# A hand-planned attention and gated-MLP kernel: set-up chain, last additions, turned tiles and the choice of plan

## Chip, core and metric

The kernel runs on one core of a Trainium2 chip. The metric is device time in microseconds of one execution. Engines are called TensorE (PE in the profile), VectorE (DVE), ScalarE (ACT), GpSimd (POOL) and SyncE (SP, which issues nearly all DMAs). PEld is TensorE's weight load.

## What is computed

Four batches, eight heads, 768 positions, head size 64. Attention keeps the keys that are among the first 8 or at most 95 positions back, with a bias by distance; its output, 768 x 512 per batch, is the x of a gated MLP with f32 weights that arrive as float64 or float32.

```python
scores = scale * q @ k.T - slope[head] * dist        # masked unless global or local
a = softmax(scores);  x = a @ v                      # (B, S, 512)
h = gelu(x @ w_in);   u, v = h[..., :512], h[..., 512:]
v_n = (v - mean(v)) / sqrt(var(v) + 1e-6) * g_ln
gated = u * (einsum('ts,bsd->btd', w_sg, v_n) + b_sg)
out = x + gated @ w_out
```

## The kernel before

**Set-up.** `n_global` and `n_local` come in one small DMA (`ni`, L621). GpSimd's iotas write position tables `rel` and `key`; VectorE makes the distance table `dist` of them (L600 to L667, bf16), and each head's bias is `dist` times a slope (L685 on VectorE or L687 on ScalarE). The framework's own scheduler orders these instructions by its timeline.

**Units.** Attention is cut into 48 units (batch, two tiles of 128 queries, pair of heads), numbered in that order with 12 per batch; a unit whose first query tile is the batch's first ("own") has fewer keys. For unit m TensorE makes the scores (`s_ps`, L714), VectorE adds the bias and takes the maximum (L745), ScalarE exponentiates (L750) into `p`, VectorE takes the reciprocal of the sums (L759). Then `p` has to be turned before it can be multiplied with v (`av`, L873). This is done in one of two ways. Units below `TURNS` turn on TensorE: a diagonal tile `diag` with the reciprocals (L777) is multiplied with `p` into two PSUM banks `tps` (L845), which ScalarE or VectorE copies to `pt` (L853, L854). The other units scale `p` (L767, four instructions, on GpSimd, ScalarE or VectorE), transpose blocks on VectorE into the single buffer `tt` (L809, two instructions), write `tt` to DRAM in four DMAs (`far`, L817), and read `far` back as `pt` in one (L821). In a step n the order is: product of unit n with v, turn of unit n+1, score of unit n+3, second part of the product of unit n.

**MLP.** Each f32 product is three matmuls over high and low halves (L413 to L415). Tiles: `v` (512 columns, then normalised and split into `z`), `u`, `mix` (with `w_sg`, giving `gt`), and `out`, whose result gets x added: the high half straight from PSUM (L524), the low half in SBUF (L526, VectorE or GpSimd), then the store (L529). Temporaries share four `t` places; all products share eight PSUM banks. In the last batch nothing but MLP products is left, and the out tiles come last: three tiles with their four terms interleaved, then the fourth.

**The plan.** Operations are listed with their possible engines, model costs and reads and writes. `due` works back from TensorE's list; `order` plays the engines forward in model time and fixes for every operation its engine and place; TensorE may take an operation up to 40 ahead of the list's head. Weights of the MLP come as 8-byte words, and are converted by ScalarE and VectorE (L565 to L577) while batch 0's attention and the first steps of batch 1 run. Constants `CALM`, `PRICE` and `EARLY` steer choices between engines. In the first 30 us TensorE fills planned gaps with empty matmuls (L364). SP's DMAs leave in the planned order. At the end every engine loads a flag (L1122).

Of the kernel before, what the change touches and what calls it, by code (L numbers as in the profile page):

```python
# [10 lines left out]
F32 = mybir.dt.float32  # L11
# [32 lines left out]
CALM, PATIENCE = 5.0, 2.0  # L44

PRICE = 0.3

EARLY = 12.0
# [5 lines left out]
TURNS = 16  # L54
# [62 lines left out]
def on_pe(busy, quarters=False):  # L117
    return "PE", busy, busy + 0.17, quarters
# [68 lines left out]
class Plan:  # L187
# [53 lines left out]
    def order(self, start):  # L241
        self.due()
# [11 lines left out]
        def due(o):  # L254
            return o.due
# [28 lines left out]
        while len(done) < len(self.ops):  # L284
            went = False
            for e in self.ENGINES:
# [14 lines left out]
                for o in can:  # L301
                    if (e == "SP" and firsts(o) and head < len(pe)
                            and o.due > max(pe[head].due, 0.0) + EARLY):
# [5 lines left out]
                    calm = o.due - (pe[head].due if head < len(pe) else 0.0) > CALM  # L309
                    lag = {w[0]: (PATIENCE if calm and w[0] != "POOL" else 0.0)  # L310
                           + (PRICE if w[0] == "DVE" else 0.0) for w in o.ways}
# [35 lines left out]
            if not went:  # L347
# [4 lines left out]
                assert nexts, "no op can go on"  # L352
                t = min(nexts) + 1e-6
        return done
# [11 lines left out]
    def emit(self, start):  # L366
# [4 lines left out]
        for o in self.order(start):  # L371
# [18 lines left out]
class Moe:  # L390
# [13 lines left out]
    def terms(self, n, cols, parts, reads, behind, after):  # L404
# [12 lines left out]
        def add(i):  # L417
# [3 lines left out]
            self.plan.op([on_pe(3 * cols * 0.000453) + (partial(put, i),)], read, [ps])  # L421
# [95 lines left out]
    def out_tile(self, x, c, m, dst):  # L517
# [3 lines left out]

        def after(ps):
            o, xm = self.temp("o", CH), x[m][c]
            op([on_dve(CH) + (lambda: nc.vector.tensor_tensor(  # L524
                o.ap, ps.ap, xm[:, 0, :].bitcast(F32), ALU.add),)], [ps, xm], [o])
            lo = lambda eng: eng.tensor_tensor(o.ap, o.ap, xm[:, 1, :].bitcast(F32), ALU.add)  # L526
            op([on_dve_sb(CH) + (lambda: lo(nc.vector),), on_pool(CH) + (lambda: lo(nc.gpsimd),)],
               [xm], [o])
# [5 lines left out]
            lambda k: [gt[c, k], (w.wout, (k, m // 2))], 1, after)  # L534
# [48 lines left out]
def local_global_attention_moe(tc, qk_in, v_in, q_t, k_t, v_n, n_gl, w_in, g_ln, w_sg_t, b_sg,  # L583
# [37 lines left out]
    nc.sync.dma_start(ni, n_gl.bitcast(I32).rearrange("(o n) -> o n", o=1).to_broadcast([P, 4]))  # L621
# [23 lines left out]
    future(rel, tmp)  # L645
# [3 lines left out]
    for base in (0, -HQ):  # L649
        nc.gpsimd.affine_select(out=ident_h, in_=ident_h, compare_op=ALU.not_equal, fill=1.0,  # L650
                                base=base, pattern=[[-1, HQ]], channel_multiplier=1)

    nv = cp.tile([P, 2, 2], F32, name="nv")
    niv = ni.rearrange("p (a w) -> p a w", w=2)
    nc.vector.scalar_tensor_tensor(nv[:, :, 0], niv[:, :, 0], 0.0, niv[:, :, 1], ALU.is_lt, ALU.add)
    nc.vector.scalar_tensor_tensor(nv[:, :, 1], nv[:, :, 0], 4294967296.0, niv[:, :, 0],
                                   ALU.mult, ALU.add)
    ng, nl = nv[:, 0, 1:2], nv[:, 1, 1:2]

    nc.vector.tensor_scalar(tmp, rel, nl, FAR, ALU.is_ge, ALU.mult)  # L660
# [609 lines left out]
```

## Time and profile before

| | |
|---|---|
| median of 3 runs | 426.41 us (426.34 to 426.92) |
| the profiled execution | 425.15 us |
| its span | 423.3 us |
| mean granted clock of TensorE | 0.997 |
| from the end of the last product to the end of the span | 6.0 us |

The profiled execution is 1.26 us below the median of the runs. Rows of the trace count from the start of the span. A timeline row gives start, duration (of the whole row, where it merges several instructions, "x4"), engine, line, operation, tiles, shapes, and in brackets the idle time of that engine before it with what ended it.

### The profile page before, as it was taken

The page shows a single profiled execution, that of the slowest core. Times are in us where ns is not written, and L with a number is a line of the kernel's source. Part 1 is how long each engine was busy: PE and PEld are TensorE (multiplying, and loading weights), DVE is VectorE, ACT ScalarE, POOL GpSimd, SP SyncE. Part 2 cuts the span into 40 slices and gives each one's busy share as a digit, 9 for nine tenths or more (in the row PEclk, how much of TensorE's full clock was granted, in tenths as well). Part 3 has the DMA queues.
Part 4 walks back from the last instruction along what each step waited for, and adds up shares of the span by engine and source line. Part 5 has one row for each costly group of instructions (what it writes and reads, how often), then busy time and mean ns, then how long its engine had stood idle before and what let it go on. Part 6 is the DMA issues. An engine that isn't in the chain of part 4 may idle for free.

```text
span 423.3 us, 13841 instructions
## 1 busy us (share of the span) xinstructions
PE 407.6 (96%) x5328; PEld 370.6 (88%) x5328; DVE 304.6 (72%) x990; ACT 235.1 (56%) x787; POOL 202.0 (48%) x312
## 2 busy tenths in 40 slices
PE   8989999899999999999999999999999999999994
PEld 8877777799888888999999888999999878999994
DVE  6887899999966879866566888966566866743343
ACT  5999989866657575654246566554245434311220
POOL 2223446668577586452545466452545443323211
PEclk9999999999999999999999999999999999999998
DMA  7656493347888776553877766463886631001002
GB/s 250 217 183 187 153 291 111 125 131 215 241 258 275 197 246 168 133 153 106 242 234 219 213 197 177 125 158 108 244 248 170 168 108 38 2 0 57 19 2 81
DMA packets 50041, 68.22 MB, mean 161 GB/s; under 512 B 5808, under 2 KB 33968, under 8 KB 49968
## 3 DMA queue, kind: packets, MB, share of 16 engines
q1 hardware_dynamic: 49968, 67.26, 54.2%
q8 instruction: 44, 0.72, 0.7%
q14 instruction: 29, 0.24, 0.2%
HBM read 48.89 MB, written 18.35 MB: 159 GB/s over the span
## 4 chain that ended last, share of the span: by engine, by line
PE 76%; DVE 9%; ACT 7%; DMA 3%; issue 2%; POOL 1%; SPq 0%; POOLq 0%; DVEq 0%
PE mm_ps L413 21%; PE mm_ps L415 19%; PE mm_ps L414 19%; PE av L873 8%; PE s_ps L714 6%; ACT p L750 3%; PE tps L845 2%; DMA far<-tt 2%; DMA stage<-in_w_sg_t_dram 1%; DVE stage L570 1%; DVE stage L572 1%; DMA ni<-in_n_gl_dram 1%; DVE p L745 1%; DVE o L524 1%; DVE tt L809 1%
## 5 line engine op out<-in xcount | busy, mean ns | idle before, releaser
L750 ACT ACTIVATE p<-p,pst 128x192 f32<-128x192 f32 x192 | 84.1, 443 | 7.4 <-DVE pst L745 6.9
L767 POOL TENSOR_SCALAR p<-p,pst 128x192 f32<-128x192 f32 (+1 forms) x128 | 56.0, 454 | 21.9 <-DVE pst L759 15.4
L413 PE MATMUL mm_ps<-wsg,z 128*128 128x384 f32 x192 | 65.1, 339 | 0.4 <-ACT pt L853 0.4
L415 PE MATMUL mm_ps<-wsg,z 128*128 128x384 f32 x192 | 64.3, 335 | 0.0
L745 DVE CUSTOM_DVE_ANT_0 p<-s_ps,bias 128x192 f32<-128x192 f32 x192 | 57.3, 340 | 9.7 <-PE s_ps L714 9.4
L414 PE MATMUL mm_ps<-wsg,z 128*128 128x384 f32 x192 | 64.3, 335 | 0.0
L873 PE MATMUL av<-pt,v 64*64 64x128 f32 (+1 forms) x1408 | 54.6, 254 | 2.6 <-DMA far<-tt 1.7
L873 PEld LDWEIGHTS av<-pt,v 64*64 64x64 f32 x1408 | 38.8, 133 | 16.8 <-issue 7.0
L526 POOL TENSOR_TENSOR o<-o,x 128x384 f32<-128x384 f32 x30 | 30.4, 1014 | 44.5 <-DVE o L524 31.9
L413 PE MATMUL mm_ps<-x,win 128*128 128x384 f32 x128 | 44.3, 346 | 0.8 <-ACT pt L853 0.8
L714 PE MATMUL s_ps<-qk 64*64 64x128 f32 (+1 forms) x1408 | 42.5, 247 | 1.7 <-issue 1.0
L413 PE MATMUL mm_ps<-gt,wout 128*128 128x384 f32 x128 | 43.0, 336 | 0.0
L415 PE MATMUL mm_ps<-gt,wout 128*128 128x384 f32 x128 | 43.0, 336 | 0.0
L415 PE MATMUL mm_ps<-x,win 128*128 128x384 f32 x128 | 42.9, 335 | 0.0
L414 PE MATMUL mm_ps<-x,win 128*128 128x384 f32 x128 | 42.8, 335 | 0.0
L414 PE MATMUL mm_ps<-gt,wout 128*128 128x384 f32 x128 | 42.8, 335 | 0.0
L506 POOL TENSOR_TENSOR y<-y,u 128x384 f32<-128x384 f32 x20 | 20.3, 1014 | 43.0 <-DVE y L503 28.2
L413 PE MATMUL mm_ps<-win,x 128*128 128x512 f32 x96 | 40.4, 421 | 0.0
L445 ACT CAST gt<-y 128x384 fp32r<-128x384 f32 x29 | 14.9, 512 | 45.9 <-DVE y L506 23.5
L714 PEld LDWEIGHTS s_ps<-qk 64*64 64x64 f32 x1408 | 37.5, 134 | 2.7 <-issue 1.3
L413 PEld LDWEIGHTS mm_ps<-wsg,z 128*128 128x128 f32 x192 | 36.0, 188 | 2.1 <-issue 1.4
L415 PE MATMUL mm_ps<-win,x 128*128 128x512 f32 x96 | 37.6, 392 | 0.0
(105 smaller groups left out, 937.7 us busy)
## 6 DMA issues: line engine op xcount, KB each, us to landing
qk<-in_qk_in_dram SPq DMA_DIRECT2D x32, 352.0 KB, 3.9
far<-tt SPq DMA_DIRECT2D x96, 96.0 KB, 2.6
pt<-far SPq DMA_DIRECT2D x24, 384.0 KB, 3.5
v<-in_v_in_dram SPq DMA_DIRECT2D x32, 256.0 KB, 3.3
out_dram<-o SPq DMA_DIRECT2D x32, 192.0 KB, 2.8
qk<-in_qk_in_dram SPq DMA_DIRECT2D x16, 288.0 KB, 3.6
v<-in_v_in_dram SPq DMA_DIRECT2D x16, 192.0 KB, 3.6
far<-tt SPq DMA_DIRECT2D x32, 80.0 KB, 1.9
```

The costliest lines, as they stand in the source:

```text
L413: mm(ps.ap, ah, bh, start=(i == 0), stop=False)
L414: mm(ps.ap, ah, bl, start=False, stop=False)
L415: mm(ps.ap, al, bh, start=False, stop=(i == n - 1))
L445: put(out[:, 0, :], src.ap)
L506: by_u = lambda eng: eng.tensor_tensor(y.ap, y.ap, gt.ap, ALU.mult)
L526: lo = lambda eng: eng.tensor_tensor(o.ap, o.ap, xm[:, 1, :].bitcast(F32), ALU.add)
L714: nc.tensor.matmul(s_ps[h][e * HQ:(e + 1) * HQ, i * W + c0:i * W + c0 + n], qk[rows, qc:qc + HQ], qk[rows, QW + k0:QW + k0 + n], start=Tru ...
L745: nc.vector.tensor_tensor_reduce(out=p[:, g, 0:nk], in0=s_ps[h][:, i * W:i * W + nk], in1=bias[:, 2 * j + h, w0:w0 + nk], op0=ALU.add, op1 ...
L750: op([on_act(nk, 0.225) + (lambda p=p, g=g, nk=nk, i=i: nc.scalar.activation(p[:, g, 0:nk], p[:, g, 0:nk], AF.Exp, bias=st[:, 0, i, g:g + ...
L767: op([on_pool_ts(nk, -0.10) + (partial(scaled, lambda o, a, c: nc.gpsimd.tensor_scalar(o, a, c, 1.0, ALU.mult, ALU.mult)),), on_act(nk, 0. ...
L845: nc.tensor.matmul(tps[r][g * HQ:(g + 1) * HQ, a * HQ:(a + 1) * HQ], pc[rows, c:c + HQ], diag[rows, 2 * i + c // W], start=True, stop=True)
L873: nc.tensor.matmul(to, v[rows, vc:vc + D], of, stop=True, skip_group_check=True, **kw)
```

## The change

`n_global` is loaded from ScalarE's queue. VectorE's set-up instructions are reworked (six of them, L660 to L665, become four) and held in one written order, with `future` first. For the out tiles of the last batch's second half, the two halves of x are added to each other once the tile's first product is issued, and the result from PSUM gets that sum in one addition. `TURNS` goes from 16 to 12. The planner draws its constants and a small noise on the due times from a seed, plans 60 times, and emits the plan that is shortest by its own model; the set-up times that it assumes are 0.7 and 0.3 us earlier for the bias and for SP.

```diff
-CALM, PATIENCE = 5.0, 2.0
-PRICE = 0.3
-EARLY = 12.0
+PLANS = 60
+CALM, PATIENCE = (3.0, 12.0), 2.0
+PRICE = (0.1, 0.4)
+EARLY = (9.0, 17.0)
+APART = 0.2
-TURNS = 16
+TURNS = 12
...
-    def order(self, start):
-        self.due()
+    def order(self, start, seed):
+        rnd = random.Random(seed)
+        calm_at, early = rnd.uniform(*CALM), rnd.uniform(*EARLY)
+        price = rnd.uniform(*PRICE)
+        for o in self.ops:
+            o.begin, o.cross, o.left = None, 0.0, len(o.before)
+            o.ready = max((b.since for b in o.bufs), default=0.0)
+            o.key = o.due + rnd.gauss(0.0, APART)
...
-        return done
+        return done, max(o.end for o in done)
...
-        for o in self.order(start):
+        self.due()
+        ends = [self.order(start, seed)[1] for seed in range(PLANS)]
+        for o in self.order(start, ends.index(min(ends)))[0]:
...
-    def out_tile(self, x, c, m, dst):
+    def out_tile(self, x, c, m, dst, last=False):
+        whole = self.temp("o", CH) if last else None
+        def ahead(first):
+            xm = x[m][c]
+            both = lambda eng: eng.tensor_tensor(whole.ap, xm[:, 0, :].bitcast(F32),
+                                                 xm[:, 1, :].bitcast(F32), ALU.add)
+            op([on_dve_sb(CH) + (lambda: both(nc.vector),),
+                on_pool(CH) + (lambda: both(nc.gpsimd),)], [xm], [whole], [first])
         def after(ps):
-            o, xm = self.temp("o", CH), x[m][c]
+            o, xm = whole or self.temp("o", CH), x[m][c]
+            with_x = lambda: o.ap if last else xm[:, 0, :].bitcast(F32)
             op([on_dve(CH) + (lambda: nc.vector.tensor_tensor(
-                o.ap, ps.ap, xm[:, 0, :].bitcast(F32), ALU.add),)], [ps, xm], [o])
+                o.ap, ps.ap, with_x(), ALU.add),)], [ps, xm], [o])
...
-    nc.sync.dma_start(ni, n_gl.bitcast(I32).rearrange("(o n) -> o n", o=1).to_broadcast([P, 4]))
+    nc.scalar.dma_start(ni, n_gl.bitcast(I32).rearrange("(o n) -> o n", o=1).to_broadcast([P, 4]))
...
-    nc.vector.tensor_scalar(tmp, rel, nl, FAR, ALU.is_ge, ALU.mult)
-    nc.vector.tensor_scalar(key, key, ng, None, ALU.is_ge)
-    nc.vector.tensor_tensor(tmp, tmp, key, ALU.mult)
-    nc.vector.tensor_scalar(rel, rel, nl, None, ALU.min)
-    nc.vector.tensor_tensor(dist[:, 0:W], rel[:, 0:W], tmp[:, 0:W], ALU.max)
-    nc.vector.tensor_tensor(dist[:, 2 * W:], rel[:, W:], tmp[:, W:], ALU.max)
+    def distances():
+        future(rel, tmp)
...
+        vec.tensor_scalar(key, key, ng, FAR, ALU.is_ge, ALU.mult)
+        vec.scalar_tensor_tensor(tmp, rel, nl, key, ALU.is_ge, ALU.mult)
+        vec.scalar_tensor_tensor(dist[:, 0:W], rel[:, 0:W], nl, tmp[:, 0:W], ALU.min, ALU.max)
+        vec.scalar_tensor_tensor(dist[:, 2 * W:], rel[:, W:], nl, tmp[:, W:], ALU.min, ALU.max)
+        for src, dst, n in ((0, HQ, P), (P, 0, HQ)):
+            vec.tensor_copy(dist[:, W + dst:W + dst + n], dist[:, src:src + n])
+
+    in_turn(distances)
...
-    dist_b.since = 6.3
+    dist_b.since = 5.6
...
-                   [[moe.out_tile(x, c, m, dst) for m in range(KD)] for c in range(NCH)])
+                   [[moe.out_tile(x, c, m, dst, b == B - 1 and c == NCH - 1) for m in range(KD)]
+                    for c in range(NCH)])
...
-    plan.emit({"POOL": 3.5, "DVE": 5.5, "ACT": 2.5, "SP": 1.0})
+    plan.emit({"POOL": 3.5, "DVE": 5.5, "ACT": 2.5, "SP": 0.7})
```

## Rows read from the trace of the kernel before

**Rows 1.** The page: busy time of each engine with its share of the span and its instructions, and the chain of work that ended last, by engine.

```profile
PE 407.6 (96%) x5328; PEld 370.6 (88%) x5328; DVE 304.6 (72%) x990; ACT 235.1 (56%) x787; POOL 202.0 (48%) x312
...
PE 76%; DVE 9%; ACT 7%; DMA 3%; issue 2%; POOL 1%; SPq 0%; POOLq 0%; DVEq 0%
```

**Rows 2.** The waits of TensorE over the whole span: who waited for whom; us in total, times, the longest.

```profile
PE tps L845 <- issue: 1.8, 3, 0.8
PE av L873 <- DMA far<-tt: 1.7, 2, 1.0
```

**Rows 3.** Busy time of each engine in four stretches: the stretch, its length, busy us (instructions) of PE, PEld, DVE, ACT and POOL, granted clock, DMA share, GB/s.

```profile
62.00:92.00 30.00, 28.05 (x366) 25.17 (x357) 27.66 (x86) 24.43 (x83) 18.09 (x24) 1.00 0.40 124
92.00:122.00 30.00, 30.00 (x325) 28.10 (x324) 28.44 (x85) 21.24 (x69) 21.73 (x30) 1.00 0.74 219
...
160.00:340.00 180.00, 180.00 (x2060) 164.94 (x2057) 129.82 (x433) 93.80 (x319) 89.68 (x145) 1.00 0.65 181
```

**Rows 4.** The timeline of the first 8 us: SP's and ScalarE's first instructions, VectorE's set-up chain (part), ScalarE's first bias.

```profile
0.73 1.28 ACT L596 ACT_TABLE_LOAD   x1 [0.73 <-PEq L1256]
0.73 0.40 SPq L621 DMA_DIRECT2D ni<-in_n_gl_dram  x1
...
3.80 0.16 DVE L655 SCALAR_TENSOR_TENSOR nv<-ni 128x2 f32<-128x2 int32 x1 [2.81 <-DMA ni<-in_n_gl_dram]
3.99 0.16 DVE L656 SCALAR_TENSOR_TENSOR nv<-nv,ni 128x2 f32<-128x2 f32 x1
4.07 0.24 DVE L600 TENSOR_SCALAR setup<-setup 128x320 bf16<-128x320 bf16 x1
...
5.18 0.33 DVE L662 TENSOR_TENSOR setup<-setup 128x320 bf16<-128x320 bf16 x1
5.42 0.30 DVE L663 TENSOR_SCALAR setup<-setup,nv 128x320 bf16<-128x320 bf16 x1
...
6.06 0.28 DVE L667 COPY dist<-dist 128x128 bf16<-128x128 bf16 x2
...
6.37 1.15 ACT L687 ACTIVATE bias<-dist 128x512 bf16<-128x512 bf16 x2 [4.15 <-DVE dist L667]
```

**Rows 5.** The timeline of the end: TensorE's last product, the two additions of the last tile, its store (SP's own timeline).

```profile
417.00 0.34 PE L415 MATMUL mm_ps<-gt,wout 128*128 128x384 f32 x1
...
417.38 0.56 DVE L524 TENSOR_TENSOR o<-mm_ps,x 128x384 f32<-128x384 f32 x1
418.07 0.99 POOL L526 TENSOR_TENSOR o<-o,x 128x384 f32<-128x384 f32 x1 [1.03 <-DVE o L524]
...
419.09 0.33 SPq L529 DMA_DIRECT2D out_dram<-o  x1
```

**Rows 6.** TensorE around the turns of units 12 to 15: one turn as a piece of the chain (start, us, what), and the four timeline rows that idle time stands before.

```profile
56.98 0.58 PE tps L845 x40
...
61.74 0.62 PE L845 MATMUL tps<-diag,p 64*64 64x64 f32 x27 [0.80 <-issue]
71.56 0.44 PE L413 MATMUL mm_ps<-x,win 128*128 128x384 f32 x1 [0.83 <-ACT pt L853]
82.86 0.77 PE L714 MATMUL s_ps<-qk 64*64 64x128 f32 x24 [0.67 <-ACT pt L853]
84.41 0.44 PE L413 MATMUL mm_ps<-wsg,z 128*128 128x384 f32 x1 [0.44 <-ACT pt L853]
```

**Rows 7.** Turns through DRAM: unit 16's write and read on SP, TensorE's rows for units 18 and 19, and the page's row of the reads (number, KB each, median us from issue to landing).

```profile
93.36 1.88 SPq L817 DMA_DIRECT2D far<-tt  x4
...
97.92 0.33 SPq L821 DMA_DIRECT2D pt<-far  x1
...
125.66 0.68 PE L873 MATMUL av<-pt,v 64*64 64x128 f32 x24 [0.95 <-DMA far<-tt]
...
132.33 0.68 PE L873 MATMUL av<-pt,v 64*64 64x128 f32 x24 [0.71 <-DMA far<-tt]
...
pt<-far SPq DMA_DIRECT2D x24, 384.0 KB, 3.5
```

**Rows 8.** Groups of instructions by line and shape, over the span: busy us, mean ns of one, idle before and what ended it.

```profile
L767 POOL TENSOR_SCALAR p<-p,pst 128x192 f32<-128x192 f32 x112 | 50.1, 464 | 21.9 <-DVE pst L759 15.4 <-DMA out_dram<-o 5.3 <-DMA stage<-in_w_out_dram 1.1
L809 DVE STREAM_TRANSPOSE tt<-p 128x384 f32<-128x384 f32 x56 | 30.9, 565 | 4.9 <-POOL p L767 2.6 <-DMA far<-tt 2.3
L432 DVE SCALAR_TENSOR_TENSOR u<-u,mm_ps 128x384 f32<-128x384 f32 x32 | 17.5, 548 | 15.8 <-ACT u L430 15.8
L432 DVE SCALAR_TENSOR_TENSOR vg<-vg,mm_ps 128x512 f32<-128x512 f32 x24 | 16.3, 683 | 7.1 <-ACT vg L430 7.1
...
L853 ACT COPY pt<-tps 128x320 f32<-128x320 f32 x15 | 5.9, 416 | 0.4 <-PE tps L845 0.4
L809 DVE STREAM_TRANSPOSE tt<-p 128x256 f32<-128x256 f32 x8 | 3.3, 411 | 0.0
```

**Rows 9.** The timeline of unit 12, from its last exponential to its product with v, and TensorE's product of unit 13 (a row merges the records of one stretch).

```profile
53.36 0.41 ACT L750 ACTIVATE p<-p,pst 128x128 f32<-128x128 f32 x1
...
54.22 0.18 DVE L759 RECIPROCAL pst<-pst 128x4 f32<-128x4 f32 x1
...
59.87 0.67 PE L873 MATMUL av<-pt,v 64*64 64x128 f32 x16
...
68.80 0.50 PE L873 MATMUL av<-pt,v 64*64 64x128 f32 x10
```

More of the change, by code (lines that the diff above doesn't have):

```diff
@@ L1 @@
 import math
+import random
 from functools import partial
@@ L239, in switch @@
         return 0.0 if was == now else TO_QUARTERS if now else FROM_QUARTERS
-    def order(self, start):
-        self.due()
+    def order(self, start, seed):
[6 more added lines that the diff above has]
+            o.key = o.due + rnd.gauss(0.0, APART)
+            for b in o.bufs:
+                b.placed = False
         free = {e: start.get(e, 0.0) for e in self.ENGINES}
@@ L254, in due @@
         def due(o):
-            return o.due
+            return o.key
         def begin(w):
@@ L302, in order @@
                     if (e == "SP" and firsts(o) and head < len(pe)
-                            and o.due > max(pe[head].due, 0.0) + EARLY):
+                            and o.due > max(pe[head].due, 0.0) + early):
                         continue
@@ L307, in order @@
                         continue
-                    calm = o.due - (pe[head].due if head < len(pe) else 0.0) > CALM
+                    calm = o.due - (pe[head].due if head < len(pe) else 0.0) > calm_at
                     lag = {w[0]: (PATIENCE if calm and w[0] != "POOL" else 0.0)
-                           + (PRICE if w[0] == "DVE" else 0.0) for w in o.ways}
+                           + (price if w[0] == "DVE" else 0.0) for w in o.ways}
                     if any(max(begin(w), t) + w[2] + lag[w[0]] < t + way[2] + lag[e]
@@ L351, in order @@
                     o.ready for e in self.ENGINES for o in wait[e] if o.ready > t]
-                assert nexts, "no op can go on"
+                if not nexts:
+                    return done, math.inf
                 t = min(nexts) + 1e-6
-        return done
+        return done, max(o.end for o in done)
     def keep_on(self, o):
@@ L370, in emit @@
                      for c in (mybir.DependencyClass.NoSync, mybir.DependencyClass.Sync))
-        for o in self.order(start):
+        self.due()
+        ends = [self.order(start, seed)[1] for seed in range(PLANS)]
+        assert min(ends) < math.inf, "no op can go on"
+        for o in self.order(start, ends.index(min(ends)))[0]:
             n = len(bb.instructions)
@@ L402, in small, with terms @@
         return Buf(lambda i: self.tp.tile([P, n], F32, tag=f"{name}{i}", name=name), name)
-    def terms(self, n, cols, parts, reads, behind, after):
+    def terms(self, n, cols, parts, reads, behind, after, ahead=None):
         ps = self.bank("mm_ps", cols, SPARE)
@@ L420, in add @@
                 read = [r for a in range(n - behind) for r in reads(a)]
-            self.plan.op([on_pe(3 * cols * 0.000453) + (partial(put, i),)], read, [ps])
+            first = self.plan.op([on_pe(3 * cols * 0.000453) + (partial(put, i),)], read, [ps])
+            if i == 0 and ahead:
+                ahead(first)
             if i == n - 1:
@@ L533, in out_tile @@
                                (gt[c, k][:, 0, :], gt[c, k][:, 1, :])),
-            lambda k: [gt[c, k], (w.wout, (k, m // 2))], 1, after)
+            lambda k: [gt[c, k], (w.wout, (k, m // 2))], 1, after, ahead if last else None)
     def run(self, x, dst):
```

26 lines of the change are left out of this document (17 added, 9 removed).

## Prediction

> **What bounds the kernel now.** I read the page first. TensorE is busy 96% of the span, VectorE 72%, ScalarE 56%; the chain that ended last runs through TensorE for 76% and through VectorE and ScalarE for 16% [rows 1]. So the second question is where TensorE is not the limit, and the waits of TensorE answer it: they are few, and the ones that matter here are its wait before the turns (`tps`) and its wait for a turned tile that comes back from DRAM [rows 2]. The windows by stage give the picture to keep: from 160 us to the end of the products TensorE has no idle time at all (180.00 of 180), while from 62 to 92 us it has 28.05 of 30 with VectorE at 27.66, and from 92 to 122 us both are full (30.00 and 28.44) [rows 3]. Work taken off TensorE is worth its full price only if VectorE's stretch up to 122 us lets it through. The timelines of the first 8 us, of the last 6 us and of the four turns in question give the prices. The profiled execution took 425.15 us, 1.85 more than its span; the median of the runs is 426.41, so I work in the span and add 3.11 (1.85 + 1.26) at the end. 0.85 us (0.2%) is about what a measurement of this kernel can tell from no change.
>
> **n_global on ACT's queue.** Now SP issues it at 0.73 us and takes 0.40 us; its data let VectorE start at 3.80 [rows 4]. ACT also begins at 0.73, with its table load of 1.28 us. If the load goes first on ACT, it lands when it does now; SP is free 0.4 us sooner for the first q, k and v, whose scores already wait for VectorE. Value: 0. The other bound: it is issued behind the table load and the first activation, about 1.5 us later. I take the first, because ACT's first instruction that needs data must wait for a memset, and the load waits for nothing.
>
> **The set-up chain.** Now it runs from 3.80 to the end of the two copies at 6.34 (6.06 + 0.28), and ACT's first bias follows at 6.37 [rows 4]. Two instructions of `future` stand in the middle of it, one of them at 4.07 for 0.24 us; in the new order they come before the number lands (their ten iotas need no DMA). Six instructions (L660 to L665) become four: key and FAR go into one tensor_scalar, and three scalar_tensor_tensor do the rest. An instruction that needs the one before starts 0.04 us after its end (L655 ends 3.96, L656 starts 3.99); L662 to L663, which need nothing of each other, overlap by 0.09. So: L656 ends 4.15; key at 4.19 for 0.30 (as L663) to 4.49; then the combined instructions. Their price in bf16 is not in the trace. Lower bound: the two-tensor rate of L662, 0.33 for 320 columns. Upper bound: scalar_tensor_tensor in f32 takes 683 ns at 512 and 548 at 384 columns [rows 8], 1.05 ns a column, hence 0.48, 0.35 and 0.28 for 320, 192 and 128. I take the upper, since it is the same operation: tmp 4.53 to 5.01, dist 5.05 to 5.40, the second overlapped, two copies 5.44 to 5.8. That is 0.5 us earlier; with the lower bound 0.85; with the late DMA above it is 1.5 - 0.5 = 1.0 later. ACT runs from the bias straight into the exponentials, so what it gets early it passes on: **-0.5**. The Trainium skill ("VectorE: DVE Perf Modes", What auto-detection actually checks) lets a two-source operation take the double rate when every tensor is 16-bit and contiguous, unless the operation's programs don't allow it. By that rule the chain would gain the 0.85 and the sum below would be -3.95 instead of -3.6; its table of rates does not list scalar_tensor_tensor, and no row of this kernel shows it in bf16.
>
> **x halves under the last products.** Now the last product ends at 417.34, VectorE adds the high half from 417.38 for 0.56, POOL adds the low half from 418.07 for 0.99, and the last store is issued at 419.09, 4.2 us before the end of the span [rows 5]. Afterwards high and low are added ahead, while the tile's products run, and one VectorE addition of the same size remains: the store can go at 417.94 + 0.03 = 417.97. **-1.1**. The four additions ahead cost VectorE 4 x 0.56 or POOL 4 x 1.0 in a stretch where both are mostly idle; each holds one of the four `t` places from its tile's first product on. Without that cover a late addition would cost the last tile at most the 1.1 again.
>
> **Twelve turns on TensorE.** Units 12 to 15 now turn through TensorE. One turn of an own unit is 40 records in 0.58 us of the chain [rows 6]; four are **-2.3**. What stood at TensorE's side of those turns: four gaps of 0.80, 0.83, 0.67 and 0.44 us, three of them ended by ScalarE's copy out of `tps` (a bank that was not free), together 2.74 [rows 6]. With the turns gone, the bank waits go, but weights still in preparation may hold the same products; bounds 0 and -2.7, I take half, **-1.4**. ScalarE and VectorE lose eight copies of about 0.42 us and POOL its diag tiles; in come, per unit, four scalings (0.46 each on POOL), two transposes on VectorE (about 0.98 with the 256-column one) and five DMA issues on SP [rows 8]. VectorE's net is at most 4 x 0.98 = +3.9 us in the stretch where it is already full.
>
> The new wait is the round trip. Unit 16's four writes start at 93.36, the read is issued at 97.92 and lands 3.5 us later: 8.1 us [rows 7]. Unit 12's last exponential starts at 53.36 and its reciprocal ends at 54.40; its product with v now starts at 59.87 [rows 9]. Scaling (1.7 on POOL), transposing (1.0) and 8.1 bring it to 65.2: 5.3 us late against the present order. Queued behind it are the score of unit 15, which the plan ties to it, and that unit's softmax; on SP the five issues stand ahead of weight loads. TensorE's cover is the two v tiles of batch 0 that are still open, eight terms at 0.70 us by the plan's own price (3 x 512 x 0.000453), 5.6 us in all: just enough. Unit 13 has more time, since its product comes 9 us later [rows 9], and so have 14 and 15. What remains uncovered I take from the nearest event: of the first turns by DMA, the third and fourth made TensorE wait 0.95 and 0.71 us [rows 7], so **+1.7**. Bounds: 0, and 5.3.
>
> **The drawn plans.** Seeds change the order of everything, at the same work. No row prices that. I put 0, with the remaining stalls as the bound below (the second 1.4 of gaps, 1.7 of far waits: -3.1), and as the bound above the same 3.1 as losses.
>
> Sum: -0.5 - 1.1 - 2.3 - 1.4 + 1.7 = -3.6. Span 423.3 - 3.6 = 419.7, which with 3.11 gives **422.8 us** on the scale of the median.
>
> **Rivals.** *A, slower: unit 12 comes late and nothing covers it.* Place: TensorE's product of unit 12 with v. For it: the 5.3 us are worked out from rows, and TensorE has to do the eight cover terms there anyhow, so a hole filled at 60 opens again before the u products, whose weights are not ready. Against: the plan sees the transfers and may reorder by 40 operations. Price: -0.5 - 1.1 - 2.3 + 5.3 = +1.4, 427.8 us. It decides from 4.75 us of uncovered wait (3.9 + 0.85); from 3.05 to 4.75 there is no change. Chance 0.20.
>
> *B: VectorE gives it back.* TensorE gets past 92 us earlier, but VectorE, 28.44 of 30 busy up to 122 us and now with up to 3.9 us more, brings the turned tiles of units 18 and 19 no sooner, and TensorE waits there longer than the 1.66 us of now. Then only start and tail are left, -1.6: 424.8 us. Against: POOL has 8 to 12 us idle in each of those two stretches [rows 3] and can take low halves from VectorE. Chance 0.20, a third of it inside 0.85 us.
>
> *C: the draw finds an order without those stalls.* -3.6 - 3.1 = -6.7: 419.7 us. For it: sixty draws; against: no row shows that their ranking by the model follows the chip. Chance 0.12.
>
> *D: the load doesn't do what it says,* standing behind ACT's table load: +1.0 in place of -0.5, so -2.1, 424.3 us. Chance 0.06.
>
> **How the numbers follow.** My forecast has 0.42, spread from 421.5 to 424. Faster by over 0.2%: 0.42 + 0.12 + 0.05 (most of D) + 0.14 (two thirds of B) = 0.73. Within 0.2%: 0.12 (the rest of B and D, a quarter of A). Slower: 0.15 (the rest of A). The range goes down to 419.0, which leaves out half of C (0.06), and up to 427.5, which leaves out most of A's slower part (0.11): 419.0 to 427.5.
>
> **What would show it.** Right: VectorE's copies of dist end near 5.8; no POOL row of `o` behind the last product, the last store about 0.03 us after the last VectorE row; `tps` has 544 records, far 144 issues; no gap ended by ScalarE's `pt` copy between 60 and 85 us; the stretch from TensorE's first u product to 417 shortens. Wrong: a gap of several us before the product of unit 12 or the first u product (A); longer `far` waits near 120 us (B); n_global's issue behind the table load (D). The prediction fails most easily on the cover of unit 12 and on what the draw does to the stretch from 60 to 135 us.

## The result: slower, 429.02 us

The changed kernel takes 429.02 us (median of 4 runs, 427.76 to 429.34) against 426.38 for the kernel before beside it (4 runs): a ratio of 1.0056, 95% interval 1.0032 to 1.0079. The forecast was 422.8, within 419.0 to 427.5; the direction was wrong. The profiled execution took 428.82 us with a span of 427.0, 3.7 more than before; the medians are 2.6 apart, since the profile before lies 1.26 us below its median and this one 0.2 below.

The page after, busy time of each engine and the chain that ended last, by engine, to be held against [rows 1]:

```profile
PE 406.8 (95%) x5183; PEld 370.3 (87%) x5183; DVE 324.1 (76%) x1042; ACT 246.3 (58%) x816; POOL 153.2 (36%) x241
...
PE 73%; DVE 9%; DMA 8%; ACT 5%; issue 2%; SPq 1%; DVEq 0%; ACTq 0%
```

TensorE has 145 records fewer, and its span is still longer: it waits. In the chain DMA went from 3% to 8%. 49 us of GpSimd's work are gone, some of it now on VectorE (+19.5) and ScalarE (+11.2). The stretches after, with the columns of [rows 3]:

```profile
62.00:92.00 30.00, 24.80 (x210) 22.29 (x209) 28.37 (x85) 23.57 (x73) 12.95 (x18) 0.94 0.62 181
92.00:122.00 30.00, 28.52 (x310) 26.82 (x310) 27.36 (x82) 21.95 (x68) 18.36 (x23) 1.00 0.73 219
...
160.00:340.00 180.00, 179.04 (x2144) 163.91 (x2142) 141.55 (x468) 102.12 (x346) 67.13 (x108) 1.00 0.66 186
```

The loss stands in the first row: from 62 to 92 us TensorE is busy 24.80 of 30 (before 28.05), the DMA share rose from 0.40 to 0.62, and the granted clock is 0.94. TensorE's waits after, from 40 to 130 us (who for whom; us, times, longest):

```profile
PE av L918 <- DMA pt<-far: 2.8, 2, 1.6
PE av L918 <- ACT z L465: 2.5, 1, 2.5
PE av L918 <- issue: 1.4, 2, 1.0
PE mm_ps L433 <- POOL win L608: 1.1, 1, 1.1
```

ScalarE's copies out of `tps` no longer make TensorE wait here, as forecast, but tiles from DRAM and weights (`win`) do. Units 12 and 13, from the reciprocal of unit 12 (56.30) and that of unit 13 (66.71) to TensorE's product of unit 13 (timeline, VectorE, GpSimd, SP and TensorE):

```profile
56.30 0.18 DVE L804 RECIPROCAL pst<-pst 128x4 f32<-128x4 f32 x1
57.11 1.18 POOL L812 TENSOR_SCALAR p<-p,pst 128x192 f32<-128x192 f32 x3
...
59.46 0.45 DVE L854 STREAM_TRANSPOSE tt<-p 128x256 f32<-128x256 f32 x1
...
59.96 2.87 SPq L862 DMA_DIRECT2D far<-tt  x4
...
66.17 0.62 SPq L866 DMA_DIRECT2D pt<-far  x1
...
66.71 0.17 DVE L804 RECIPROCAL pst<-pst 128x4 f32<-128x4 f32 x1
68.85 0.90 DVE L854 STREAM_TRANSPOSE tt<-p 128x384 f32<-128x384 f32 x2
...
69.67 0.50 PE L918 MATMUL av<-pt,v 64*64 64x128 f32 x10 [1.59 <-DMA pt<-far]
69.77 1.93 SPq L862 DMA_DIRECT2D far<-tt  x4
71.75 2.64 SPq L593 DMA_DIRECT2D stage<-in_w_in_dram  x4
74.48 0.38 SPq L589 DMA_DIRECT2D stage<-in_w_sg_t_dram  x1
74.99 0.52 SPq L866 DMA_DIRECT2D pt<-far  x1
...
80.42 0.80 PE L918 MATMUL av<-pt,v 64*64 64x128 f32 x10 [2.53 <-ACT z L465]
```

And unit 13's reciprocal in the kernel before (timeline, VectorE):

```profile
59.16 0.17 DVE L759 RECIPROCAL pst<-pst 128x4 f32<-128x4 f32 x1
```

Unit 12's trip takes from 59.96 to 69.63, 9.7 us where I had 8.1, and its product comes at 69.67 (before 59.87). Unit 13's softmax comes late: its reciprocal stands 10.4 us behind unit 12's, where before it was 4.9 us (54.22 and 59.16). The single `tt` isn't what holds it, since unit 12's last write had landed at 66.08. VectorE transposes at 68.85, the last write lands at 74.92, and the read, issued at 74.99, lands 5.34 us later at 80.33: 10.6 us for this trip, 13.5 from reciprocal to tile. The product starts 0.09 us after that landing. The releaser named in the last row, `z`, ended 0.2 us before it and is no input of the product (`av<-pt,v`), so I read this too as a wait for DRAM. Then the clock (stretches before, in and behind the drop; columns as above):

```profile
76.80:80.20 3.40, 1.09 (x7) 0.77 (x5) 2.88 (x9) 2.87 (x9) 1.41 (x2) 1.00 1.03 343
80.20:83.60 3.40, 3.18 (x57) 2.88 (x58) 2.46 (x9) 1.26 (x4) 0.00 (x0) 0.50 0.45 158
83.60:87.00 3.40, 3.40 (x21) 3.40 (x21) 3.40 (x9) 3.01 (x10) 2.68 (x4) 1.00 0.24 82
```

After a stretch with 1.09 us of work in 3.40, TensorE ran 3.4 us at 1.2 GHz: its 3.18 busy us there are worth about 1.6 at 2.4 GHz (an estimate: half of them). In these 10.2 us the wait cost twice.

The set-up after (timeline of the first 8 us; ScalarE, VectorE and ScalarE's queue), against [rows 4]:

```profile
0.73 0.40 ACTq L652 DMA_DIRECT2D ni<-in_n_gl_dram  x1
...
1.17 1.28 ACT L627 ACT_TABLE_LOAD   x1 [1.17 <-PEq L1302]
...
5.49 0.16 DVE L701 SCALAR_TENSOR_TENSOR nv<-ni 128x2 f32<-128x2 int32 x1 [2.31 <-DMA ni<-in_n_gl_dram]
...
6.30 0.55 DVE L706 SCALAR_TENSOR_TENSOR setup<-setup,nv 128x320 bf16<-128x320 bf16 x1
...
6.88 0.42 DVE L707 SCALAR_TENSOR_TENSOR dist<-setup,nv 128x192 bf16<-128x192 bf16 x1
7.22 0.35 DVE L708 SCALAR_TENSOR_TENSOR dist<-setup,nv 128x128 bf16<-128x128 bf16 x1
7.48 0.28 DVE L710 COPY dist<-dist 128x128 bf16<-128x128 bf16 x2
...
7.79 0.63 ACT L732 ACTIVATE bias<-dist 128x512 bf16<-128x512 bf16 x1 [5.13 <-DVE dist L710]
```

And the load's row among the DMA issues of that stretch (number, KB, us from issue to landing):

```profile
ni<-in_n_gl_dram ACTq DMA_DIRECT2D x1, 2.0 KB, 4.7
```

The load goes out at 0.73 as I had it, ahead of the table load, and lands 4.73 us later, not 3.04: the first bias comes at 7.79 instead of 6.37. The end (TensorE's last matmul, the one addition behind it), against [rows 5]:

```profile
421.67 0.34 PE L433 MATMUL mm_ps<-gt,wout 128*128 128x384 f32 x1
422.05 0.56 DVE L554 TENSOR_TENSOR o<-mm_ps,o 128x384 f32<-128x384 f32 x1 [1.06 <-PE mm_ps L433]
```

From the end of the last product (422.01) to the end of the span it is 5.04 us, before 5.95. The last store is issued 0.62 us behind the last product instead of 1.75.

**How the traces are compared below.** A later start shifts every later time, so I read from each trace when TensorE has done the same amount of useful work: scores, products with v and MLP products, counted from the matmul records at full-clock prices, turns and empty matmuls left out. Four such points are P1 to P4; the kernel before passes them at 51.51, 63.38, 83.23 and 226.59 us. The table gives each kernel's time minus these, TensorE's busy time from 62 to 92 us, its DMA share, and the median. Runs of one kernel lie some 4 us apart (the kernel before: 424.4 to 428.25 us in 29 runs on one chip), and the intervals of the ratios are 0.25 to 0.5% wide on either side, so a difference of medians below 1 to 2 us isn't told apart. The points are read from one execution each, which need not be a typical one (e12's took 429.16 us, its slowest run); e11_t16 and e19_best are the same kernel on two chips and differ by up to 1.0 us there.

| kernel | turns on TensorE | P1 | P2 | P3 | P4 | PE busy | DMA | median |
|---|---|---|---|---|---|---|---|---|
| after | 12 | +1.91 | +0.46 | +4.30 | +4.67 | 24.80 | 0.62 | 429.02 |
| e1_ni_sp | 12 | -0.25 | -3.04 | +0.79 | +0.67 | 23.14 | 0.63 | 426.76 |
| e5_turns12_alone | 12 | -0.54 | -3.33 | +2.16 | +1.87 | 24.80 | 0.53 | 427.21 |
| e12_t12_seed10 | 12 | +1.30 | -1.27 | +1.15 | +4.70 | 24.09 | 0.63 | 426.48 |
| e13_t12_seed55 | 12 | +2.76 | -0.06 | +5.34 | +3.73 | 24.17 | 0.64 | 430.90 |
| e8_no_trip | 12 | +0.66 | -0.75 | +0.87 | +1.04 | 26.82 | 0.67 | 426.70 |
| e9_wires | 12 | +0.51 | -0.29 | +1.56 | -0.16 | 25.90 | 0.67 | 423.70 |
| e4_draw_alone | 16 | +0.07 | +3.21 | +3.74 | +0.99 | 28.14 | 0.39 | 426.32 |
| e6_chain_tail | 16 | -0.11 | +0.51 | +0.50 | +2.27 | 27.81 | 0.39 | 426.04 |
| e11_t16 | 16 | +1.15 | +0.53 | -0.07 | -1.20 | 29.48 | 0.41 | 423.12 |
| e14_t16_seed31 | 16 | +0.37 | +0.41 | +4.67 | +1.98 | 26.33 | 0.39 | 426.91 |
| e15_t16_wires | 16 | -0.30 | +1.21 | -0.87 | -1.53 | 28.56 | 0.40 | 423.96 |
| e19_best | 16 | +1.52 | +1.53 | +0.83 | -1.07 | 29.25 | 0.42 | 423.42 |

### The profile page after: what moved, and what is told of

It is laid out like the page before. It is cut to its first block, busy times and chain, and to the rows that moved or that the text cites. A ratio compares the mean times of both kernels' runs of the same rounds, so it can differ in the third digit from the quotient of the medians.

```text
span 427.0 us, 13587 instructions
## 1 busy us (share of the span) xinstructions
PE 406.8 (95%) x5183; PEld 370.3 (87%) x5183; DVE 324.1 (76%) x1042; ACT 246.3 (58%) x816; POOL 153.2 (36%) x241
## 4 chain that ended last, share of the span: by engine, by line
PE 73%; DVE 9%; DMA 8%; ACT 5%; issue 2%; SPq 1%; DVEq 0%; ACTq 0%
PE mm_ps L431 21%; PE mm_ps L433 19%; PE mm_ps L432 19%; PE av L918 8%; PE s_ps L759 6%; DMA pt<-far 2%; ACT p L795 2%; DMA far<-tt 2%; PE tps L890 1%; DVE tt L854 1%; DMA v<-in_v_in_dram 1%; DMA ni<-in_n_gl_dram 1%; DMA stage<-in_w_sg_t_dram 1%; DVE p L790 1%; SPq L862 1%
## 5 line engine op out<-in xcount | busy, mean ns | idle before, releaser
L795 ACT ACTIVATE p<-p,pst 128x192 f32<-128x192 f32 (+1 forms) x192 | 84.2, 444 | 12.4 <-DVE pst L790 10.3
L790 DVE CUSTOM_DVE_ANT_0 p<-s_ps,bias 128x192 f32<-128x192 f32 (+1 forms) x192 | 57.2, 339 | 11.8 <-PE s_ps L759 11.6
L918 PE MATMUL av<-pt,v 64*64 64x128 f32 (+1 forms) x1408 | 56.0, 256 | 9.8 <-DMA pt<-far 3.4
L812 POOL TENSOR_SCALAR p<-p,pst 128x192 f32<-128x192 f32 (+1 forms) x89 | 41.1, 475 | 64.4 <-DVE pst L804 54.0
L918 PEld LDWEIGHTS av<-pt,v 64*64 64x64 f32 x1408 | 39.8, 135 | 24.6 <-issue 10.0
L759 PE MATMUL s_ps<-qk 64*64 64x64 f32 (+1 forms) x1408 | 43.1, 251 | 0.9 <-DMA qk<-in_qk_in_dram 0.8
L557 POOL TENSOR_TENSOR o<-o,x 128x384 f32<-128x384 f32 x26 | 26.4, 1016 | 42.1 <-DVE o L554 30.2
L431 PE MATMUL mm_ps<-win,x 128*128 128x512 f32 x96 | 40.3, 420 | 0.0
L854 DVE STREAM_TRANSPOSE tt<-p 128x384 f32<-128x384 f32 (+1 forms) x72 | 36.8, 537 | 3.0 <-DMA far<-tt 1.5
L433 PE MATMUL mm_ps<-win,x 128*128 128x512 f32 x96 | 37.8, 393 | 0.0
L432 PE MATMUL mm_ps<-win,x 128*128 128x512 f32 x96 | 37.6, 392 | 0.0
```

The lines of the kernel that those rows point to most:

```text
L431: mm(ps.ap, ah, bh, start=(i == 0), stop=False)
L432: mm(ps.ap, ah, bl, start=False, stop=False)
L433: mm(ps.ap, al, bh, start=False, stop=(i == n - 1))
L759: nc.tensor.matmul(s_ps[h][e * HQ:(e + 1) * HQ, i * W + c0:i * W + c0 + n], qk[rows, qc:qc + HQ], qk[rows, QW + k0:QW + k0 + n], start=Tru ...
L790: nc.vector.tensor_tensor_reduce(out=p[:, g, 0:nk], in0=s_ps[h][:, i * W:i * W + nk], in1=bias[:, 2 * j + h, w0:w0 + nk], op0=ALU.add, op1 ...
L795: op([on_act(nk, 0.225) + (lambda p=p, g=g, nk=nk, i=i: nc.scalar.activation(p[:, g, 0:nk], p[:, g, 0:nk], AF.Exp, bias=st[:, 0, i, g:g + ...
```

## Experiments: each part by itself

Theory: twelve turns win on TensorE what was forecast, and the round trips of units 12 and 13 take it back, with the late load on top. Rivals: the draw picked a bad order; VectorE holds the stretch. Four kernels on one chip.

**e1_ni_sp**

```diff
-    nc.scalar.dma_start(ni, n_gl...
+    nc.sync.dma_start(ni, n_gl...
```

> The changed kernel with one edit taken back: n_global is loaded from SP's queue, first, as before; plan, twelve turns, set-up order and last additions stay, so the order on every engine is that of the changed kernel. Theory 'the load on ACT's queue delays the start': the load lands at 3.8 us and not at 5.5, the bias starts near 6.1 (7.8 in the changed kernel, 6.4 before), and if the start carries through, the time falls by 1.4 to 1.7 us, to 427.3 to 427.6. Theory 'TensorE's waits between 60 and 90 us set the end whatever the start': the waits there grow by what the start gives, and the time stays at 428.5 to 429.3.

426.76 us, ratio 1.0014 (0.9978 to 1.005). The first bias comes at 6.36, and with the same order TensorE is 3.04 us ahead at P2; at P3 it is 0.79 behind, after waits of 2.50, 1.10 and 3.06 us. From P2 to P3 it loses 3.83 us, as much as the changed kernel (3.84). The clock didn't fall before the end in this profile (mean 0.998), but ten of the twelve runs have a mean of 0.988 to 0.995 (the changed kernel's profile, with one drop, has 0.994). The profiles differ by 2.2 us at P1 and 3.5 at P3, where unit 13's tile lands 2.0 us later in the changed kernel (80.33 against 78.30) and the clock falls behind it. So in these profiles the late start is carried that far; in the medians it isn't shown, since the two intervals overlap. The twelve turns gain nothing even without it.

**e5_turns12_alone**

```diff
-TURNS = 16
+TURNS = 12      # in the kernel before
```

> The kernel before with one edit: TURNS 12, planned with the constants of before. Theory 'the turns are the loss': TensorE waits for the tiles of units 12 and 13 from DRAM and for what follows, 3 us or more more between 60 and 90 us than the 2.7 us of before, time 428 to 430. Theory 'the drawn plan is the loss': the four turns are hidden, TensorE saves its 2.3 us, time 423 to 425.

427.21 us, ratio 1.0036 (1.0004 to 1.0067). TensorE's longest wait from 40 to 130 us (who for whom; us, times, longest), and the stretch with the columns of [rows 3]:

```profile
PE av L904 <- DMA pt<-far: 4.7, 2, 2.7
```

```profile
62.00:92.00 30.00, 24.80 (x207) 22.82 (x206) 26.63 (x84) 22.15 (x69) 20.07 (x27) 0.89 0.53 154
```

3.33 us ahead at P2, 2.16 behind at P3: two waits for tiles from DRAM, 2.03 and 2.66 us, each followed by 3.4 us at a clock of 0.5 (hence 0.89). It is this edit, with nothing drawn, that loses 5.5 us there. The time lies between the two theories' ranges: the turns gain nothing, and they lose less than the theory said.

**e6_chain_tail**: the kernel before with the set-up order and the x halves alone.

> The kernel before with only the set-up order (n_global on SP's queue) and the x halves under the last products; plan constants, sixteen turns and planned times as before, so that all else stands in the same order. By the two steps of the prediction: bias 0.3 to 0.5 us earlier than 6.37, end of the last product to end of span 5.0 us in place of 6.0; time 424.9 to 425.4. If the start does not carry, 425.4. If both are hidden or the late additions hold something up, 426.4.

426.04 us, ratio 0.9987 (0.996 to 1.0014). The first bias is 0.14 us earlier. The last store is issued 0.62 us behind the last product instead of 1.75, but it took 3.62 us to land (2.44 before), and the end behind the last product is 6.01 us, no shorter than before. And from 118 to 138 us it lost 1.4 us more than the kernel before, at waits for tiles from DRAM (0.76 and 1.46 us) in an order that is the same: such waits differ from execution to execution.

**e4_draw_alone**: the kernel before with the sixty plans alone (16 turns).

> The kernel before with one edit: sixty plans are drawn and the model's shortest is taken (sixteen turns, set-up and end as before). Theory 'the drawn plan is the loss': 428 to 430, with work moved from POOL to VectorE and waits of TensorE at places that had none. Theory 'the turns are the loss': the draw is neutral or better, 424.5 to 426.5.

426.32 us, ratio 1.0009 (0.9975 to 1.0044). Its plan has a wait of 2.15 us at 57.9 with 3.4 us at a clock of 0.5 behind it (+3.21 at P2), and makes it up later. The draw by itself neither gained nor lost.

## Experiments: the load, the trip, the plan

**e7_head_start**

```diff
     nc.scalar.dma_start(ni, n_gl...
+    ni2 = dp.tile([P, 4], I32, name="ni2")
+    nc.sync.dma_start(ni2, n_gl...
```

> The kernel after, with one more small load: SyncE's queue first issues the same broadcast of n_global and n_local (to a scrap place in DRAM) and only then its first q, k and v loads. So n_global stays on ScalarE's queue, and SyncE's large loads start some 0.4 us later, as they did in the kernel before. If n_global came late (4.73 us after its issue) because its small packets share the DMA engines with large loads issued at the same moment, it lands 3.0 to 3.6 us after its issue and VectorE's chain starts near 4.0 to 4.4. If ScalarE's queue itself is the slow one (its place beside the table load, or the queue's own start), it lands 4.5 to 5 us after its issue and the chain starts at 5.3 to 5.6 as in the kernel after.

One run, 427.51 us. The load's row among the DMA issues of the first 8 us (us to landing last), and in the timeline VectorE's first use and the first bias:

```profile
ni<-in_n_gl_dram ACTq DMA_DIRECT2D x1, 2.0 KB, 2.6
```

```profile
3.33 0.16 DVE L703 SCALAR_TENSOR_TENSOR nv<-ni 128x2 f32<-128x2 int32 x1
...
5.64 1.15 ACT L734 ACTIVATE bias<-dist 128x512 bf16<-128x512 bf16 x2 [3.00 <-DVE dist L712]
```

On the same queue the load now lands 2.6 us after its issue, earlier than in any other run. So ScalarE's queue by itself is not slow: in the changed kernel the load's 144 small packets ran beside SP's large loads issued at the same 0.73 us, here those go out at 1.43. The Trainium skill ("DMA: Bandwidth & Descriptors", Issuing engines are not separate DMA queues) has transfers that ScalarE, SyncE or GpSimd issue interleave on the same 16 DMA engines. The landings fit that (4.73 against 2.6 us), but don't show which engines carried the packets. Here q and k pay, the first score coming 2.1 us later than before (6.91 against 4.81).

**e8_no_trip**

```diff
+        near = lambda: qk_in[b, j, u][:, 0:Q4 * nt * QB].rearrange("p (a f) -> p a f", a=Q4)
+        back = lambda: near() if n < 16 else far[...]
-            to[:, :, 0:nt * QB], far[...])
+            to[:, :, 0:nt * QB], back())
```

> The changed kernel with n_global on SyncE's queue, every instruction in the same order, but the read of a turned tile for units 12 to 15 takes its bytes from the q, k input in DRAM instead of from the tile just written, so that it waits for no write (the result of these units is left wrong; sizes are the same). Theory 1, the round trip through DRAM is what eats the lead of about 3 us that TensorE has at 60 us: the waits of 2.5 us near 67 and 3 us near 78 go or shrink below 1 us each, TensorE is still 2 to 3 us ahead of the kernel before at equal work at 85 us, and the time is about 3 us under that of the order with the trip: 423.5 us. Rival, VectorE and the weights hold the stretch from 62 to 92 us anyhow: the gaps come back as waits for z, for converted weights or for VectorE's products, TensorE is level at 85 us, and the time stays at 426.3 to 427.

426.70 us, ratio 0.9996 (0.9961 to 1.003): the theory's 423.5 did not come. TensorE's waits from 40 to 130 us:

```profile
PE mm_ps L433 <- POOL win L608: 2.0, 1, 2.0
PE av L920 <- DMA pt<-far: 1.7, 1, 1.7
PE av L920 <- issue: 1.5, 2, 1.0
PE av L920 <- ACT z L465: 1.0, 1, 1.0
```

The waits for units 12 and 13 are down from 2.5 and 3.1 us to at most 1.0 (the 1.7 is a unit that still goes through `far`, at 117 us). But the edit is only a small part of that. On SP the reads keep their places: unit 12's tile lands at 65.84 (e1 67.04), and unit 13's read, behind the weight loads as in e1, is issued at 73.08 and lands at 78.39 (e1 73.01 and 78.30). The waits are shorter because TensorE comes later, after a wait of 1.01 us at 56.5 that e1 doesn't have and one of 2.00 for a converted weight (`win`, on GpSimd) at 70.8, with 3.4 us of half clock behind it; at P3 it stands level with e1 (+0.87, +0.79). So this run doesn't decide whether the wait for the write is what eats the lead. It shows that unit 13's tile comes no sooner without that wait.

**e9_wires**

```diff
-        op([("SP", Q4 * 0.38, P * nt * P * 4 / 300e3, there)], [tt], [far])
+        op([("SP", Q4 * 0.38, P * nt * P * 4 / 220e3, there)], [tt], [far])
...
-    wire = lambda words: ("SP", 0.38, P * words * 4 / 360e3)   # and two more like it
+    wire = lambda words: ("SP", 0.38, P * words * 4 / 260e3)
```

> The changed kernel with n_global on SyncE's queue, 12 turns, and the plan made with dearer transfers: the rates in the planner's price of a DMA go from 300 and 360 to 220 and 260 bytes per ns, since the trace shows 181 to 219 GB/s moved and 4 to 5 us from issue to landing where loads, writes and reads meet. Theory 1: the planner put the products of units 12 and 13 where they wait because it priced the round trip too low; with the dearer price the waits for tiles from DRAM between 60 and 85 us shrink below 1 us each, and the time falls by 1.5 to 3 us against the same kernel with the old price: 424 to 425.3 us. Rival: there is no work to put ahead of them, so the waits stay in sum or go to other places; 426 to 428 us.

423.70 us, ratio 0.9923 (0.9895 to 0.9952), faster than before with the same twelve turns. From P2 to P3 it loses 1.85 us, and behind P3 it gains 1.7. Unit 13's tile lands at 78.18, about when it does in e1, but here TensorE has work almost until then and waits 0.37 us for it. A wait of 1.23 for unit 12 remains, against the expectation, and a drop of the clock (at 70.9, after that wait and one of 1.38 us). What it shows for certain is that twelve turns are not slow in every order. That the dearer transfers are why is not shown, since the planner then also draws another seed (14).

**e11_t16**: `TURNS = 16`, and n_global on SP's queue; seed 48 is drawn.

> The changed kernel with n_global on SyncE's queue and 16 turns on TensorE again (the draw then picks another of its sixty plans). So the set-up order, the x halves and the draw are left. Theory 1 (what was gained by 12 turns is lost at the round trips): TensorE has no lead at 60 us and loses none until 85 us; no gap of 2 to 3 us for a tile from DRAM between 62 and 85; the time is like that of 12 turns within 0.8 us, 425.5 to 426.5. Rival (12 turns are what makes the kernel slow as a whole): 424 to 425, at least 1.5 us below 12 turns with the same load queue.

423.12 us, ratio 0.9905 (0.9869 to 0.9941). TensorE's stretch:

```profile
62.00:92.00 30.00, 29.48 (x378) 25.81 (x379) 28.26 (x89) 26.11 (x84) 14.13 (x19) 1.00 0.41 123
```

Busy 29.48 of 30 with VectorE as full as ever: VectorE's load alone doesn't hold this stretch. The DMA share is 0.41 against 0.62, but that isn't shown to be the difference: e9_wires is as fast with 0.67, and e14_t16_seed31 slow with 0.39. The rival of the expectation (at least 1.5 us below twelve turns) is what came, and lower than its range; the run below with another seed shows that the sixteen turns aren't the reason by themselves.

**e12_t12_seed10, e13_t12_seed55, e14_t16_seed31**: other seeds than the planner's first.

```diff
-        for o in self.order(start, ends.index(min(ends)))[0]:
+        for o in self.order(start, 10)[0]:      # 55; 31 with TURNS = 16
```

> The changed kernel with n_global on SyncE's queue and the plan of seed 10, which the planner ranks second at 12 turns (CALM drawn as 8.1 instead of 11.2, EARLY 12.4 instead of 10.1); same work. Theory of the round trip: at 12 turns with the planner's cheap transfers any plan makes TensorE wait for units 12 and 13 or for what is queued behind their transfers, so 2 to 4 us are lost between 60 and 88 us and the time stays at 426 to 427.5. Rival, the one plan that was drawn: the order is what differs, not the turns; another plan of nearly the same rank is off by 2 us or more, below 425.

> As the run before it, with seed 55, ranked third (CALM 3.8, EARLY 16.6, PRICE 0.14: GpSimd takes more from VectorE and loads go earlier). Theory of the round trip: 426 to 427.5, with waits for tiles from DRAM between 60 and 88 us. The one plan that was drawn: below 425, and GpSimd busier than 15 of 30 us between 62 and 92.

> The changed kernel with n_global on SyncE's queue, 16 turns, and the plan of seed 31, which the planner ranks second there (0.02 us behind seed 48 by its model). If 16 turns keep TensorE free of the waits for DRAM whatever the plan, it comes within 1 us of seed 48's 423.12. If seed 48 was luck of the draw, it comes out at 425 or more, as the undrawn plan with the same edits did (426.04).

426.48 (ratio 1.0006, 0.9982 to 1.0031), 430.90 (1.0109, 1.006 to 1.0158) and 426.91 us (1.0045, 1.0012 to 1.0078). At twelve turns with the old price no plan that was run gets below 426.4, and in all of them TensorE is idle 5 to 7 us from 62 to 92. e13's stretch:

```profile
62.00:92.00 30.00, 24.17 (x201) 20.78 (x202) 27.60 (x82) 22.35 (x72) 22.88 (x29) 0.94 0.64 179
```

GpSimd took 22.88 us of work there, as expected of its constants, and it is the slowest of all, outside both ranges of the expectation. At 16 turns seed 31, second by the planner's model, is 3.8 us slower than seed 48 (on another chip; by the ratios 1.0045 and 0.9905): two waits of its own (2.14 us behind the guard, an empty instruction that frees a product with v, 1.38 for `diag`) and 6.8 us of half clock. So in these pairs the ranking of the planner doesn't carry to the chip.

**e15_t16_wires**: 16 turns and the dearer transfers.

> The changed kernel with n_global on SyncE's queue, 16 turns, and the dearer transfers in the planner's prices (220 and 260 bytes per ns). If the price of transfers mattered only through the round trips of units 12 to 15, it changes little here: 422.5 to 424. If it mends the order of loads as a whole (the weights that TensorE waits for around 60 to 90 us and the waits between 120 and 160), it is below 422.5.

423.96 us, ratio 0.9956 (0.9922 to 0.999): within what was expected of a price that matters for the trips alone.

## Experiments: one plan, one part at a time

All with 16 turns and seed 48, on one chip: e19_best is e11_t16 again, and the others each differ from it in one part (the diffs are those of the change, taken back or put in).

> The kernel of 16 turns with the changed chain, the changed tail, the plan of seed 48 and n_global on SyncE's queue, beside the three that each undo or redo one part of it. Theory: its plan is good on the chip again, 0.988 to 0.993 of the kernel before, and the lowest of the four. Rival: its earlier time was favoured by having been picked: 0.994 to 1.0.

> 16 turns and the plan of seed 48 in all four kernels of this call; the changed set-up chain and the x halves as in the changed kernel; here alone n_global is loaded by ScalarE's queue. Theory: the load lands some 1.5 us later and the first bias comes 1.4 us later, TensorE in the first 30 us has idle time that is filled by empty matmuls, and ScalarE runs from the bias straight into the exponentials, so the delay is carried to the end: 1.4 us above the same kernel with SyncE's queue. Rival: the slack of the first 60 us swallows it: within 0.5 us.

> 16 turns, the plan of seed 48, n_global on SyncE's queue, the changed set-up chain; the last out tiles add the two halves of x one after the other as in the kernel before (one more row on GpSimd behind the last product). Theory: 1.0 us above the same kernel with the changed tail, seen as 5.9 instead of 5.0 us from the end of the last product to the end of the span. Rival: the store's own landing hides it, within 0.5 us.

> 16 turns, the plan of seed 48, n_global on SyncE's queue, the changed tail; VectorE's set-up chain as in the kernel before. Theory, by the 2.27 against 2.54 us that the chain took from its load to the copies: the first bias 0.2 to 0.3 us later and the time 0.3 us above the same kernel with the new chain, which is little to see in a median. Rival (the combined instructions are worth what I had predicted): 0.5 to 0.85 us.

e19_best: 423.42 us, ratio 0.9928 (0.9902 to 0.9953), faster than both kernels, though not the lowest of the four. e17_old_tail (old additions): 424.62, 0.9964 (0.994 to 0.9988), 1.2 us more; in the profiles its end behind the last product is 0.90 longer (6.43 against 5.53; span +0.4, though its P4 is 0.47 earlier). e16_act_queue: 424.09, 0.9967 (0.9945 to 0.9989). e18_old_chain: 422.29, 0.9916 (0.9887 to 0.9946), not slower but 1.1 lower, within the overlap of the intervals. The first bias in e19_best and in e16_act_queue:

```profile
6.18 1.15 ACT L732 ACTIVATE bias<-dist 128x512 bf16<-128x512 bf16 x2 [3.95 <-DVE dist L710]
```

```profile
7.79 1.15 ACT L732 ACTIVATE bias<-dist 128x512 bf16<-128x512 bf16 x2 [5.13 <-DVE dist L710]
```

ScalarE starts 1.61 us later; TensorE is 1.12 later at 41 us (42.00 against 40.88), 0.08 later at P2, and earlier at P4 (-1.65 against -1.07). In these two profiles the late start is swallowed before 63 us: e19_best waits 0.99 us for a score at 48.4 that e16_act_queue doesn't wait for. Against e11_t16, the same kernel as e19_best, it is still 1.1 us at P2, and the medians (0.67 apart) decide between neither theory. In the changed kernel's own plan moving the load back gave 1.0014 for 1.0056, on another chip; what part of those 1.8 us is the late load stays open.

## Why the prediction was wrong

**"Unit 13 has more time, since its product comes 9 us later": this step failed.** It put unit 13's wait at nothing, and that was 2.53 us (2.66 in e5, 3.06 in e1), the longest of all. I never did for unit 13 the sum that I did for unit 12. In the kernel before its reciprocal ends at 59.33; with the 1.7, 1.0 and 8.1 of the prediction the tile is there at 70.1, already 1.3 us behind its product at 68.80. On the chip the reciprocal itself moved to 66.71, the trip took 10.6 us, and the tile landed at 80.33. The read alone took 5.34 us, with a DMA share of 0.90 from 74 to 78 us; in e1 the weight loads on SP held it 1.1 us more (last write landed 71.93, read issued 73.01), in the changed kernel they didn't.

**The new wait, unit 12 (+1.7, bounds 0 and 5.3): right in number, by luck.** TensorE waited 1.59 us (2.03 and 2.50 in e5 and e1). But the reciprocal came 2.1 us later than before, the trip took 9.7 us instead of 8.1, and the tile landed at 69.63 where I had 65.2; TensorE was later too. I had taken the trip from 92 to 102 us, where the DMA share was 0.69; from 58 to 62 us, when unit 12's writes went out, it was 0.97.

**The clock wasn't in the sum.** A gap of 2 to 3 us here was followed by 3.4 us at 1.2 GHz in the changed kernel, and twice in e5, an estimated 1.6 us more each. I had priced a gap at its length.

**Turns and bank waits (-3.7): right in kind, its size not measured by itself.** The bank waits went. e1 and e5 are 3.0 and 3.3 us ahead at P2, where the turns of units 12 and 13 and one of the four gaps lie behind; counted in the same way, e1 and the changed kernel gain another 1.5 on the kernel before from 81 to 84 us, past the turn of unit 15. In the changed kernel the lead at P2 is hidden under the late start.

**Rival A, at 0.20, was nearest.** It put 5.3 us on unit 12; in the changed kernel the waits from 62 to 83 us are 1.59 for unit 12, 1.09 for a weight and 2.53 for unit 13, with about 1.6 for the clock. These don't close a sum: less the forecast 3.7 on the turns and the 0.9 at the end, and with 1.4 for the late bias, they give +3.6, near the +3.7 of the span, but the same sum gives e1 +2.1, and its span is 0.1 longer than before. Rival B added nothing: from P3 to P4 the changed kernel loses 0.37 us.

**n_global (0; other bound +1.5 - 0.5): the bound's size was right, its cause wrong.** The load was not behind the table load but beside SP's large loads; the bias came 1.42 us later.

**The chain (-0.5): half.** From the load's landing to the end of the copies it takes 2.27 us instead of 2.54, 0.27 less. The combined instructions cost 0.55, 0.42 and 0.35 us at 320, 192 and 128 columns, above my upper bound (0.48, 0.35, 0.28), whose slope of 1.05 ns a column was right and which had no fixed part. The Trainium skill's double rate for 16-bit operands ("VectorE: DVE Perf Modes", What auto-detection actually checks) is not what these rows show for scalar_tensor_tensor, whose per-partition scalar is f32: 128 more columns cost 0.13 us, where the two-tensor operations of before (0.33 us at 320, 0.26 at 192) take 0.07. In the end the chain is worth nothing that can be measured (e18).

**The tail (-1.1): right up to the store.** It is issued 1.1 us earlier in every profile with the new tail. What reaches the end of the span depends on how long that store takes to land (1.9 to 3.6 us) and on what follows: 0.91 in the changed kernel's profile, 0.90 between e17 and e19, nothing in e6.

**The draw (0, ±3.1): too narrow, and wrong as a side matter.** Plans that the model ranks first and second (16 turns) or second and third (12 turns) lie 3.8 and 4.4 us apart on the chip, and e13 is 4.3 above the kernel before. Rival C's 3 us are there, for one of the six seeds that were run at the old price (48).

What stays open: whether the dearer transfers or a lucky seed made e9_wires good, what the wait for the write is worth by itself (e8 doesn't tell), why unit 13's softmax comes so late in the drawn order (VectorE, busy 4.00 of 4 us from 62 to 66, is likely but not tested), and the late load's share of the measured time.

## What to carry to other kernels

When work is moved from a busy engine to a round trip through memory, do the sum for each unit that makes the trip and not for the first alone: from when its input is ready, not from how late its result is due. A price taken from a stretch with fewer transfers can be too low (here 8.1 for 9.7 and 10.6 us). Allow for what the clock may take after an uncovered wait. And a plan picked by a model from sixty is worth as much as the model's order of them: time a few of its best on the chip before you believe the first.

## What the runs showed that I had not expected

A load of 2 KB in 144 packets took 2.6, 3.04 or 4.73 us to land, with different loads issued beside it. TensorE's granted clock fell to 0.5 for 3.4 us behind a gap of 2.53 us in the changed kernel, of 2.03 and 2.66 in e5_turns12_alone, of 1.23 and 1.38 in e9_wires; the profile of e1_ni_sp has gaps of 2.50 and 3.06 us and no drop. And a lead that TensorE has before a tile from DRAM is lost in the wait for it: e1 and e8 pass P2 2.3 us apart and P3 level, 0.1 us apart, with unit 13's tile landing at 78.30 and 78.39.
